# Warm-up matmuls, an earlier row load past a branch, a first block whose rows come a unit sooner, and small groups' weight loads spread two per block

## The chip, the cores and the metric

The kernel runs on one core of one Trainium2 chip. The metric is device time in microseconds (us) of one execution, lower is better. Five engines work side by side, each through its own list of instructions in order: TensorE (PE in the profile; PEld is its weight load), VectorE (DVE), ScalarE (ACT), GpSimd (POOL) and SyncE (SP), which here issues nearly all transfers between DRAM and the on-chip memory. ACTq, SPq and PEq are the engines' sequencers, which issue DMAs and take branches.

## The reference

Three layers follow one another on 4608 tokens of 512 values.

```python
# 1. linear attention: batch 8, heads 8, 576 tokens, head size 64, 128 features
proj = q_or_k @ w_phi                       # w_phi 64x128
proj = proj - max(abs(proj), axis=-1)
phi = concat([exp(proj), exp(-proj)])       # 256 features
kv = einsum('bhsf,bhsd->bhfd', phi_k, v); z = sum(phi_k, axis=seq)
num = phi_q @ kv; den = phi_q @ z + 1e-6    # attention = num / den -> x (4608, 512)
# 2. mixture of experts, top 1 of 8
logits = x @ w_gate + modality_bias[modality_id]
e_idx = argmax(logits); gate_w = softmax(logits)[e_idx]
for e in range(8):
    out[mask] = gate_w[mask] * (relu(x[mask] @ w1[e]) @ w2[e])   # w1 512x1024, w2 1024x512
# 3. a dense layer with a SoLU and a layer norm
h = out @ w_in                              # 512x1024
solu = h * softmax(h)
ln = (solu - mean(solu)) / sqrt(var(solu) + 1e-6) * g_ln
return ln @ w_out                           # 1024x512
```

## The kernel before

**Arithmetic.** Most products are made of three matmuls: each float32 operand is split into a high part (a rounding copy by ACT: `hi`, `whi`, `yTh`) and the low rest (a subtraction by DVE or POOL: `lo`, `wlo`, `yTl`), and high·high, low·high and high·low are added up (the helper at L1075 to L1078, `mm3`). An operand can be used once its copy and its rest are there.

**Stages.** The attention runs first, to some 430 us. ACT loads `w_phi` by two DMAs (L72, L73) and splits it (L76, L77); PE turns blocks of q and k (L255, `tp<-ident,ldk`), ACT and DVE split them (L258, L259), and L267 to L269 project them. Gates and routing write each token's row into `xe` in DRAM, sorted by expert. The experts work in nineteen units `u` = 0 to 18 of up to 256 rows. A unit's rows (`xin`) are read from `xe`, turned and split, multiplied with the first weights (`mm1`), passed through relu, multiplied with the second weights (`mm2`) and stored turned to `yd`. Its weights come as eight loads of 512 KB (`ldk`, `ldq`, `ldv`), asked for by SP in the order in which buffers come free, then split. Leftovers go into four small groups of 32 rows (`quad()`), of which each step multiplies with eight weight chunks' worth of a float32 copy without a split; their 24 later chunks are loaded by `load_mini`.

**Branch.** After units 0 and 1, `extras(0)` (L1468 to L1478) holds code for experts with too many rows. Its branch `tc.If(more > j)` is not taken with these inputs. Every engine must pass it; behind it SP waits for a buffer (`used((1, 7))`), loads the last chunk and then unit 3's rows (`m.load_x(3)`, L913, with the gates at L923).

**Dense layer.** The 36 tiles of 128 tokens go through `block()`: split of the next rows (`yT`, ACT L926 and POOL L927), the load of rows further on (`load_y`: `yin` L1226, `gt` L1228), `a3(n)` (24 matmuls of 128x512 with `win`, softmax, norm), turning of the result by DVE and a round trip through DRAM (`turned` L1244, `wlo` L1248, both issued by SP; the second waits for the first to land), `lnT` and the split of that (ACT `whi` L1297), and `a4`, the product with `w_out`, three tiles behind. `a3(0)` runs at the end of the last unit (u = 18, `NU-1`); then eight steps of `quad` stand between blocks, two blocks to a step. `w_in` and `w_out` are split by a generator `bg`, whose 66 steps are spread over `NPREP` uses of weights. The rows of the first two tiles are loaded with `load_y(0)` at the end of unit 17.

**Order.** PE's order is written by hand in the attention and from the units on; in the units the other engines' order is too. SP issues transfers in the order written there and stops at the first that must wait.

Of the kernel before, what the change touches and what calls it, by code (L numbers as in the profile page):

```python
# [39 lines left out]
COLS64 = 2  # L40
COLS32 = 1
TAIL = 1
BIAS = 8
BGN = 1
BGP = 100
PRE = 2
FSTEP = 2
RING = 5
RING0 = 1
STEP0 = 6  # L50
# [13 lines left out]
def setup_consts(nc, keep, pool, w_phi, w_gate):  # L64
    V, G = nc.vector, nc.gpsimd
    c = Consts()
    c.ident = keep.tile([P, P], F32, name="ident")
    make_identity(nc, c.ident)

# [1 line left out]
    V.memset(raw, 0.0)  # L71
    nc.scalar.dma_start(out=raw[0:D, 0:F], in_=w_phi)  # L72
    nc.scalar.dma_start(out=raw[D:P, F : 2 * F], in_=w_phi)  # L73
    c.wphi_hi = pool.tile([P, 2 * F], F32R, name="wphi_hi")
    c.wphi_lo = pool.tile([P, 2 * F], F32R, name="wphi_lo")
    nc.scalar.copy(c.wphi_hi, raw)  # L76
# [117 lines left out]
def attention(ctx, tc, c, cnt, xe, q, k, v, ld, early, m, late):  # L194
# [10 lines left out]
    kvp = ctx.enter_context(tc.tile_pool(name="a_kv", bufs=1, space=PSUM))  # L205

    ctx.enter_context(tc.manual_schedule(engines={mybir.EngineType.PE}))
    gd = [w1p.tile([P, 2, 4, 32], F32, name=f"gd{i}") for i in range(2)]
    for g_ in gd:
        V.memset(g_, 0.0)  # L210
# [745 lines left out]
def moe(ctx, m):  # L956
# [92 lines left out]
    def load_mini(i, g):  # L1049
        e, _, _, on = regs[NU + g]  # L1050
        m.load_raw(i, e, on != 0, i % 2 * NMINI + g)
# [3 lines left out]
    done = [RING0]  # L1055
    uses, steps_done = [0], [0]
    NSTEP = 4 * (2 * KD + KF) + 2
    NPREP = 8 * (START - 3) - 6

    def split_to(j):  # L1060
        while done[0] <= min(j, len(order) - 1):
# [170 lines left out]
    def yT(i):  # L1232
        hi = p2.tile([P, KD, P], F32R, name="yTh")
        lo = p2.tile([P, KD, P], F32R, name="yTl")
        m.split(ys[i][0], hi, lo, G)
        yt[i] = (hi, lo)
# [13 lines left out]
    def a3(i):  # L1250
        h = hps.tile([P, 2, 2, 2 * P], F32, name="h2").rearrange("p a b t -> p (a b t)")
        y = yt.pop(i)
        sc = lambda nm: p2.tile([P, 1], F32, name="s_" + nm)
        halves = [slice(n * 512, (n + 1) * 512) for n in range(2)]
        mxs = [sc("mx0"), sc("mx1")]
        for sl in halves:
            for k in range(KD):
                mm3(h[:, sl], both(y, lambda t: t[:, k, :]), both(win[k], lambda t: t[:, sl]), k == 0, k == KD - 1)
        for sl, mx in zip(halves, mxs):
            V.tensor_reduce(out=mx, in_=h[:, sl], axis=AX.X, op=ALU.max, negate=True)  # L1260
        g = ys[i][1]
        V.scalar_tensor_tensor(out=mx, in0=mx, scalar=mxs[0], in1=g, op0=ALU.min, op1=ALU.mult)
        ex = p1.tile([P, DFF], F32, name="ex")
        sm = sc("sm")
        A.activation(ex, h, AF.Exp, bias=mx, scale=g, accum_out=sm)  # L1265
        r = sc("r")
        V.tensor_scalar(out=r, in0=sm, scalar1=1e-9, scalar2=None, op0=ALU.add)
        V.reciprocal(r, r)
        tot = sc("tot")
        V.scalar_tensor_tensor(out=ex, in0=ex, scalar=r, in1=h, op0=ALU.mult, op1=ALU.mult, accum_out=tot)  # L1270
        for sl in halves:
            V.tensor_scalar(out=ex[:, sl], in0=ex[:, sl], scalar1=float(DFF), scalar2=tot, op0=ALU.mult, op1=ALU.subtract)  # L1272
        sq = p1.tile([P, DFF], BF16, name="sq")
        var = p2.tile([P, 1], F32, name="s_var")
        A.activation(sq, ex, AF.Square, accum_out=var)  # L1275
        rs = p2.tile([P, 1], F32, name="rs", bufs=5)
        g = ys[i][1]
        G.tensor_scalar(out=rs, in0=var, scalar1=g, scalar2=g, op0=ALU.mult, op1=ALU.mult)
        G.tensor_scalar(out=rs, in0=rs, scalar1=float(DFF) ** -3, scalar2=1e-6, op0=ALU.mult, op1=ALU.add)
        G.tensor_tensor(out=rs, in0=rs, in1=c.mhalf, op=ALU.pow)  # L1280
        G.tensor_scalar(out=rs, in0=rs, scalar1=g, scalar2=1.0 / DFF, op0=ALU.mult, op1=ALU.mult)
        st["rs", i] = rs
        st[i] = ex
        if i < NT - 1:
            st["lo", i] = lo = rp.tile([P, DFF], F32R, name="wlo")
            turn(i, ex, lo)
# [70 lines left out]
    def quad():  # L1357
        us = range(NU, NU + NMINI)
        group = lambda g: slice(g * MINI, (g + 1) * MINI)

        x = p1.tile([P, 2, DM], F32, name="xin")[:, 0, :]
        for g, u in enumerate(us):
            SP.dma_start(out=x[group(g)], in_=m.xe[bass.ds(regs[u][1], MINI), 0:DM])
            m.keep_gates(u)
        yield
        xt = blocks(x, KD, [m.xtp.tile([P, 4, P], F32, name="xTh")])[0]
        yield
        for i in range(4):
            if i % 2 == 0:
                b = bank.tile([P, 2, 2 * P], F32, name="tp")  # L1370
            for f in range(4):
                for g in range(NMINI):
                    T.matmul(
                        b[group(g), i % 2, :], lhsT=xt[:, f, group(g)], rhs=m.w1c(i % 2 * NMINI + g)[:, f, :],
                        start=i % 2 == f == 0, stop=f == 3, tile_position=(0, g * MINI), skip_group_check=True,
                    )
            for g in range(NMINI):
                load_mini(i + 2, g)
            if i % 2:
                A.activation(m.hr[:, i // 2 * 512 : i // 2 * 512 + 512], b.rearrange("p a f -> p (a f)"), AF.Relu)  # L1380
            yield
        ht = blocks(m.hr, KF, [p1.tile([P, 4, P], F32, name=f"hTh{n}") for n in range(2)])
        b = bank.tile([P, 2, 2 * P], F32, name="tp")
        yield
        for j in range(4):
            fh, dh = j // 2, j % 2
            for f in range(4):
                for g in range(NMINI):
                    T.matmul(  # L1389
                        b[group(g), dh, :], lhsT=ht[fh][:, f, group(g)], rhs=m.w1c(j % 2 * NMINI + g)[:, f, :],  # L1390
                        start=j == f == 0, stop=fh == 1 and f == 3, tile_position=(0, g * MINI), skip_group_check=True,
                    )
            if j < 2:
                for g in range(NMINI):
                    load_mini(j + 6, g)
            yield
        yr = p1.tile([P, DM], F32, name="yr")
        A.copy(yr, b.rearrange("p a d -> p (a d)"))
        yield
        yo = blocks(yr, KD, [p2.tile([P, 4, P], F32, name="yo")])[0]  # L1400

        def store(g, u):
            SP.dma_start(
                out=yd[:, m.cols(u)].rearrange("(c p) t -> p c t", p=P), in_=yo[:, :, group(g)]
            )
            slots[0] += g == NMINI - 1

        stores.extend(lambda g=g, u=u: store(g, u) for g, u in enumerate(us))
        yield
# [17 lines left out]

    def unit(u):
        gap(u)
        g = mm1(u)  # L1430
        for i in range(4):
            next(g)
            if i == XAT:
                run_mids()
                next_x(u)
                if u == NU - 2:
                    next(minis)
        run(g)
        gap(u)
        if u == NU - 2:  # L1440
            run(bg)
            load_y(0)
        if u == NU - 1:
            yT(0)
            next(minis)
            run_mids()
            block()
        run_mids()
        run(mm2([u]))

    with ExitStack() as sp:
        sp.enter_context(tc.manual_schedule(engines={mybir.EngineType.SP} | MANUAL))
        slot_regs(2, then=lambda: m.load_x(2, False))
        m.keep_gates(2)
        slot_regs(3)
        for ch in order[:RING0]:
            reload(*ch)
        split_to(LOOK)
        ln = tr(m.hr, ("yin", "ex"), p1)
        hT[0] = lambda f: both(ln, lambda t: t[:, f, :])  # L1460
        g = mm1(1)
        run(g)
        for i, _ in enumerate(mm2([0, 1])):
            if i == 2:
                m.xT(bank, 2)
        held = mids[:]
        mids.clear()
    more = nc.values_load(tab[0:1, 4:5], min_val=0, max_val=NEXTRA)  # L1468
# [12 lines left out]
    mids.extend(held)  # L1481
    ctx.enter_context(tc.manual_schedule(engines={mybir.EngineType.SP}))
    used((1, 7))
    m.load_x(3)
    slot_regs(4)
    nxt = [0, 0, 0]
    stores = []

    def block():
        n, split, done4 = nxt  # L1490
        run_mids()
        if n + 1 < NT:
            yT(n + 1)
            if n == 0:
                load_y(1)
            elif n % 2 and n + 3 < NT:
                load_y((n + 3) // 2)
            elif stores:
                stores.pop(0)()
        if n == NT - 1:  # L1500
            lnT(split)
        if n < NT:
            a3(n)
            nxt[0] += 1
        if split < n - 1:
            if n < NT - 1:
                lnT(split)
            nxt[1] += 1
        if done4 < n - 2:
            a4(done4)  # L1510
            nxt[2] += 1

    def gap(u):
        if u >= START:
            block()
# [105 lines left out]
```

## Time and profile before

| what | value |
| --- | --- |
| three runs, median | 1294.19 us (1291.05 to 1295.75) |
| profiled execution | 1293.31 us |
| its span in the trace | 1291.6 us (1.7 us lie around it) |
| mean granted clock of TensorE | 0.996 |
| busy PE / DVE / ACT / POOL | 98% / 67% / 52% / 31% |

The span runs from the first to the last instruction of the trace. A time in a row is counted from the span's start. Idle time of an engine stands in brackets behind the row of the instruction that ended it, with the one that released it.

### The profile page before, as it was taken

What the parts mean: (1) busy time and instruction counts of PE and PEld (TensorE: products, weight loads), DVE (VectorE), ACT (ScalarE), POOL (GpSimd) and SP (SyncE); (2) the same over time, 40 slices, a digit from 0 to 9 for tenths busy, and PEclk for the clock granted to TensorE, in tenths of its full rate; (3) what the DMA queues carried; (4) which work ended last, traced back from release to release, by engine and by line L of the source; (5) the groups of instructions that cost most, each with busy time, mean ns of one, the idle gap of its engine ahead of it and who ended that gap; (6) DMA issues with size and microseconds to landing.
All of it is one profiled execution on the core that took longest, in us unless ns stands there. A gap on an engine that the chain in (4) does not pass through costs nothing.

```text
span 1291.6 us, 25365 instructions
## 1 busy us (share of the span) xinstructions
PE 1260.4 (98%) x9242; PEld 1057.8 (82%) x9242; DVE 869.3 (67%) x1620; ACT 666.8 (52%) x1254; POOL 403.8 (31%) x479
## 2 busy tenths in 40 slices
PE   8999999999999989999999999999999999999997
PEld 7767777777766889999999999987777778888885
DVE  8757866876775848778878787747555555566562
ACT  5666666666665426555555555534334434444442
POOL 6655674674663200000000000013323323333331
PEclk9999999999999999999999999999999999999999
DMA  8711342232132222222623132477877875566542
GB/s 246 214 54 58 107 133 58 87 117 85 50 116 67 91 67 92 67 83 66 197 66 83 51 83 67 130 213 192 233 204 168 248 169 142 137 153 139 145 121 57
DMA packets 273760, 156.78 MB, mean 121 GB/s; under 512 B 181824, under 2 KB 255712, under 8 KB 273632
## 3 DMA queue, kind: packets, MB, share of 16 engines
q1 hardware_dynamic: 267648, 136.01, 39.3%
q0 software_dynamic: 5824, 19.04, 3.8%
q8 instruction: 75, 1.23, 0.4%
q14 instruction: 53, 0.43, 0.1%
q10 hardware_dynamic: 160, 0.07, 0.0%
HBM read 166.67 MB, written 51.37 MB: 169 GB/s over the span
## 4 chain that ended last, share of the span: by engine, by line
PE 53%; DMA 5%; SPq 2%; issue 1%; ACT 1%; DVE 1%; POOL 0%; POOLq 0%; ACTq 0%; DVEq 0%
PE tp L1078 26%; PE h L1078 25%; DMA turned<-whi 2%; PE tp L898 1%; DMA gd<-xe 1%; SPq L1248 1%; DMA wlo<-turned 1%; PE tp L1389 1%; SPq L884 1%; DMA yin<-yd 0%; ACT ex L1265 0%; DVE ex L1270 0%; DMA xin<-xe 0%; ACT whi L1297 0%; SPq L1228 0%
## 5 line engine op out<-in xcount | busy, mean ns | idle before, releaser
L322 POOL TENSOR_TENSOR es<-es,e 128x512 f32<-128x512 f32 x128 | 163.8, 1286 | 102.5 <-ACT e L278 90.9
L927 POOL TENSOR_TENSOR yTl<-yin,yTh 128x512 fp32r<-128x512 f32 x36 | 46.8, 1300 | 443.2 <-ACT yTh L926 442.1
L1078 PE MATMUL tp<-xTh,whi 128*128 128x256 f32 x432 | 121.7, 282 | 2.5 <-PEq L1470 2.1
L1078 PE MATMUL h<-hTl,whi 128*128 128x256 f32 x432 | 120.6, 279 | 0.4 <-DVE hTl L1093 0.4
L1078 PE MATMUL tp<-xTh,wlo 128*128 128x256 f32 x432 | 120.6, 279 | 0.0
L1078 PE MATMUL tp<-xTl,whi 128*128 128x256 f32 x432 | 120.5, 279 | 0.0
L1078 PE MATMUL h<-hTh,whi 128*128 128x256 f32 x432 | 120.5, 279 | 0.0
L1078 PE MATMUL h<-hTh,wlo 128*128 128x256 f32 x432 | 120.5, 279 | 0.0
L271 DVE TENSOR_REDUCE m<-mm 128x4 f32<-128x512 f32 x144 | 97.1, 681 | 15.9 <-PE mm L269 15.9
L259 DVE TENSOR_TENSOR lo<-tp,hi 128x512 fp32r<-128x512 f32 x72 | 49.6, 689 | 82.5 <-ACT hi L258 82.0
L1265 ACT ACTIVATE ex<-h,s_mx,gt 128x1024 f32<-128x1024 f32 x36 | 43.4, 1207 | 111.6 <-issue 56.8
L1260 DVE TENSOR_REDUCE s_mx<-h 128x1 f32<-128x512 f32 x72 | 46.3, 685 | 80.6 <-PE h L1078 80.6
L267 PE MATMUL mm<-wphi_hi,hi 128*128 128x256 f32 x288 | 94.2, 327 | 1.0 <-ACT hi L258 1.0
L1275 ACT ACTIVATE sq<-ex 128x1024 bf16<-128x1024 f32 x36 | 38.1, 1058 | 97.9 <-DVE ex L1272 97.9
L1078 PEld LDWEIGHTS tp<-xTh,whi 128*128 128x128 f32 x432 | 81.3, 188 | 2.9 <-issue 2.2
L338 ACT ACTIVATE qp<-tp 128x512 f32<-128x512 f32 x128 | 69.3, 597 | 25.8 <-PE tp L330 22.7
L1078 PEld LDWEIGHTS tp<-xTh,wlo 128*128 128x128 f32 x432 | 81.9, 190 | 0.0
L1078 PEld LDWEIGHTS h<-hTh,wlo 128*128 128x128 f32 x432 | 81.9, 190 | 0.0
L268 PE MATMUL mm<-wphi_lo,hi 128*128 128x256 f32 x288 | 81.6, 283 | 0.0
L1078 PEld LDWEIGHTS h<-hTl,whi 128*128 128x128 f32 x432 | 81.1, 188 | 0.6 <-DVE hTl L1093 0.6
L269 PE MATMUL mm<-wphi_hi,lo 128*128 128x256 f32 x288 | 81.4, 283 | 0.0
L1078 PEld LDWEIGHTS h<-hTh,whi 128*128 128x128 f32 x432 | 81.3, 188 | 0.0
(427 smaller groups left out, 3818.9 us busy)
## 6 DMA issues: line engine op xcount, KB each, us to landing
ldk<-in_moe_w_dram SPq DMA_DIRECT2D x66, 512.0 KB
ldv<-in_moe_w_dram SPq DMA_DIRECT2D x66, 512.0 KB
ldq<-in_moe_w_dram SPq DMA_DIRECT2D x44, 512.0 KB
turned<-whi SPq DMA_DIRECT2D x35, 512.0 KB
wlo<-turned SPq DMA_DIRECT2D x140, 128.0 KB
yd<-yo SPq DMA_DIRECT2D x36, 256.0 KB
yin<-yd SPq DMA_DIRECT2D x18, 512.0 KB
xin<-xe SPq DMA_DIRECT2D x16, 512.0 KB
```

The lines of the kernel that those rows point to most:

```text
L259: V.tensor_tensor(out=lo, in0=tp, in1=hi.bitcast(F32), op=ALU.subtract)
L267: T.matmul(o, lhsT=hi[:, 2 * a + j, :], rhs=c.wphi_hi, start=(j == 0), stop=False, skip_group_check=True)
L268: T.matmul(o, lhsT=hi[:, 2 * a + j, :], rhs=c.wphi_lo, start=False, stop=False, skip_group_check=True)
L269: T.matmul(o, lhsT=lo[:, 2 * a + j, :], rhs=c.wphi_hi, start=False, stop=True, skip_group_check=True)
L271: V.tensor_reduce(out=m, in_=pj, axis=AX.X, op=ALU.max, apply_absolute_value=True)
L322: G.tensor_tensor(out=eo, in0=eo, in1=ev[:, :, r, :], op=ALU.add)
L338: A.activation(u.qp[half][:, fh, 2 * hp : 2 * hp + 2, o : o + 2 * P], tp.rearrange("p (h r) t -> p h (r t)", r=2), AF.Exp, scale=sc,)
L927: eng.tensor_tensor(out=lo, in0=src, in1=hi.bitcast(F32), op=ALU.subtract)
L1078: T.matmul(o, lhsT=l, rhs=r, start=first and n == 0, stop=last and n == 2, skip_group_check=True)
L1260: V.tensor_reduce(out=mx, in_=h[:, sl], axis=AX.X, op=ALU.max, negate=True)
L1265: A.activation(ex, h, AF.Exp, bias=mx, scale=g, accum_out=sm)
L1275: A.activation(sq, ex, AF.Square, accum_out=var)
```

## The change

The change has six parts. (1) Twelve bf16 matmuls of zeros, 128x256, stand first on PE; DVE clears their operand (`warm`) first. (2) ACT copies one column of it (`early`), so that the load of its function table stands ahead of the two `w_phi` DMAs. (3) The list of constants that DVE works on between projections is started by another count (`BIAS`); in DVE's list the nine rows of it stand at the same place (71 and 72). (4) Unit 3's rows are asked for ahead of the branch, their gates still behind it. (5) `load_y(0)` stands at the end of unit 16 instead of 17 and the 66 splitting steps of `bg` are spread over 114 uses instead of 122; `yT(0)` stands at the start of the last unit; in `a3(0)` what is left in `mids` (pieces of turning and splitting) is run between the two halves of 12 matmuls. (6) The small groups' loads go into a list, from which each block takes two, where four were issued at once behind a step.

```diff
-BIAS = 8
+BIAS = 14
+WARM = 12
 ...
+    c.warm = pool.tile([P, 2 * P], BF16, name="warm")
+    V.memset(c.warm, 0.0)
 ...
     nc.scalar.dma_start(out=raw[0:D, 0:F], in_=w_phi)
     nc.scalar.dma_start(out=raw[D:P, F : 2 * F], in_=w_phi)
+    early = pool.tile([P, 64], F32, name="early")
+    nc.scalar.copy(early[:, 0:1], c.warm[:, 0:1])
 ...
     ctx.enter_context(tc.manual_schedule(engines={mybir.EngineType.PE}))
+    warm = mmp.tile([P, 4, F], F32, name="mm").rearrange("p a f -> p (a f)")[:, 0 : 2 * P]
+    for n in range(WARM):
+        T.matmul(warm, lhsT=c.warm[:, 0:P], rhs=c.warm, start=True, stop=True, skip_group_check=True)
 ...
-    NPREP = 8 * (START - 3) - 6
+    NPREP = 8 * (START - 4) - 6
 ...
-        for sl in halves:
+        for n, sl in enumerate(halves):
+            if i == 0 and n:
+                run_mids()
             for k in range(KD):
                 mm3(h[:, sl], both(y, lambda t: t[:, k, :]), both(win[k], lambda t: t[:, sl]), k == 0, k == KD - 1)
 ...
-            for g in range(NMINI):
-                load_mini(i + 2, g)
+            feed.extend((i + 2, g) for g in range(NMINI))
 ...
             if j < 2:
-                for g in range(NMINI):
-                    load_mini(j + 6, g)
+                feed.extend((j + 6, g) for g in range(NMINI))
 ...
     def unit(u):
         gap(u)
+        if u == NU - 1:
+            yT(0)
 ...
-        if u == NU - 2:
+        if u == NU - 3:
             run(bg)
             load_y(0)
         if u == NU - 1:
-            yT(0)
             next(minis)
-            run_mids()
-            block()
+            block(False)
         run_mids()
 ...
+        m.load_x(3, False)
         held = mids[:]
 ...
-    m.load_x(3)
+    m.keep_gates(3)
 ...
-    def block():
+    def block(mid=True):
         n, split, done4 = nxt
-        run_mids()
+        if mid:
+            run_mids()
 ...
             a3(n)
             nxt[0] += 1
+            for x in [feed.pop(0) for _ in range(2) if feed]:
+                load_mini(*x)
```

Line numbers of the changed kernel are a few higher (L255 becomes L263, L884 becomes L892, L1078 becomes L1086, L1226 becomes L1234, L1470 becomes L1481). ACT's list at the very start (`wphi_raw` is `w_phi` as loaded, `hi` the high part of a turned block), before:

```order
L72 DMA wphi_raw<-in_w_phi_dram 64x128
L73 DMA wphi_raw<-in_w_phi_dram 64x128
L76 ACT_TABLE_LOAD
L76 CAST wphi_hi<-wphi_raw 128x256
L258 CAST hi<-tp 128x512 x3
```

and after:

```order
L78 ACT_TABLE_LOAD
L78 CAST early<-warm 128x1
L75 DMA wphi_raw<-in_w_phi_dram 64x128
L76 DMA wphi_raw<-in_w_phi_dram 64x128
L81 CAST wphi_hi<-wphi_raw 128x256
L266 CAST hi<-tp 128x512 x3
```

The table load moved from behind the two DMAs to ahead of them. SP's list behind the branch (`ldk` is a weight chunk, `xin` unit 3's rows, `gd` gates), before:

```order
L1470 UNCONDITIONAL_BRANCH x2
L884 ISA
L884 REGISTER_ALU
L884 ISA
L884 DMA ldk<-in_moe_w_dram 128x4x256
L913 ISA
L913 DMA xin<-xe 128x2x512
L923 ISA
L923 DMA gd<-xe 256x2
```

and SP's list ahead of the same branch, after:

```order
L892 ISA
L892 REGISTER_ALU
L892 ISA
L892 DMA ldv<-in_moe_w_dram 128x4x256
L921 ISA
L921 DMA xin<-xe 128x2x512
L1481 COMPARE_AND_BRANCH
```

The rows' load moved past the branch and past the weight chunk `ldk`. PE's list in the last unit (`whi,xTl` ends `mm1` of unit 18, `xin` are the small groups' rows, `tp<-ident,ldq` turns relu's result of unit 18, `h` is `a3(0)`), before:

```order
L1078 MATMUL tp<-whi,xTl 128x256
L1320 MATMUL tp<-ident,xin 128x128 x4
L1115 MATMUL tp<-ident,ldq 128x128 x8
L1078 MATMUL h_12838<-win0h,yTh 128x512
L1078 MATMUL h_12838<-win0l,yTh 128x512
L1078 MATMUL h_12838<-win0h,yTl 128x512
L1078 MATMUL h_12838<-win1h,yTh 128x512
```

and after, from the end of the first half of `a3(0)` on:

```order
L1086 MATMUL h_12837<-win3h,yTh 128x512
L1086 MATMUL h_12837<-win3l,yTh 128x512
L1086 MATMUL h_12837<-win3h,yTl 128x512
L1123 MATMUL tp<-ident,ldq 128x128 x8
L1086 MATMUL h_12837<-win0h,yTh 128x512
L1086 MATMUL h_12837<-win0l,yTh 128x512
L1086 MATMUL h_12837<-win0h,yTl 128x512
```

The eight turning matmuls moved from ahead of the 24 to between the halves. SP's list in the stretch of the small groups (`turned` and `wlo` are the two legs of the round trip), before:

```order
L884 DMA ldk<-in_moe_w_dram 128x4x256
L884 ISA
L884 REGISTER_ALU
L884 ISA
L884 DMA ldv<-in_moe_w_dram 128x4x256
L1226 DMA yin<-yd 128x4x256
L1228 DMA gt<-gd 128x2x2
L1244 DMA turned_6220<-whi 128x1024
L1248 DMA wlo<-turned_6220 32x32x32 x4
L1244 DMA turned_6221<-whi 128x1024
L1248 DMA wlo<-turned_6221 32x32x32 x4
```

and after:

```order
L1236 DMA gt<-gd 128x2x2
L1252 DMA turned_6237<-whi 128x1024
L1256 DMA wlo<-turned_6237 32x32x32 x4
L892 ISA
L892 REGISTER_ALU
L892 ISA
L892 DMA ldv<-in_moe_w_dram 128x4x256
L892 ISA
L892 REGISTER_ALU
L892 ISA
L892 DMA ldk<-in_moe_w_dram 128x4x256
L1252 DMA turned_6238<-whi 128x1024
```

Two of the four loads moved from ahead of the first round trip to between the first and the second.

## Rows read from the trace of the kernel before

**Rows 1.** The page, busy time of the engines: us (share) x instructions.

```profile
PE 1260.4 (98%) x9242; PEld 1057.8 (82%) x9242; DVE 869.3 (67%) x1620; ACT 666.8 (52%) x1254; POOL 403.8 (31%) x479
```

**Rows 2.** Waits of PE: what waited, its releaser: us, times, longest.

```profile
PE tp L255 <- DMA ldk<-in_k_dram: 4.0, 1, 4.0
PE tp L1078 <- ACT whi L1297: 2.9, 4, 1.7
PE tp L898 <- DMA xin<-xe: 2.2, 1, 2.2
...
PE h L1078 <- ACT yTh L926: 1.7, 1, 1.7
```

**Rows 3.** Timeline of the start: start, us, engine, line, operation [idle before, releaser].

```profile
1.82 0.61 ACTq L73 DMA_DIRECT2D wphi_raw<-in_w_phi_dram  x1
...
5.16 1.28 ACT L76 ACT_TABLE_LOAD   x1 [5.16 <-DMA wphi_raw<-in_w_phi_dram]
...
6.46 0.41 ACT L76 CAST wphi_hi<-wphi_raw 128x256 fp32r<-128x256 f32 x1
...
7.40 0.58 PE L267 MATMUL mm<-wphi_hi,hi 128*128 128x256 f32 x1 [0.99 <-ACT hi L258]
...
10.09 0.41 PE L268 MATMUL mm<-wphi_lo,hi 128*128 128x256 f32 x1
10.30 0.42 PE L269 MATMUL mm<-wphi_hi,lo 128*128 128x256 f32 x1
...
14.87 0.28 PE L268 MATMUL mm<-wphi_lo,hi 128*128 128x256 f32 x1
14.98 0.28 PE L269 MATMUL mm<-wphi_hi,lo 128*128 128x256 f32 x1
```

**Rows 4.** Windows: length, busy PE, PEld, DVE, ACT, POOL, granted clock, DMA, GB/s.

```profile
7.40:14.00 6.60, 6.58 (x29) 6.28 (x30) 6.50 (x33) 2.06 (x4) 1.99 (x10) 1.00 0.98 245
...
478.21:481.62 3.41, 3.41 (x19) 3.41 (x17) 0.00 (x0) 0.00 (x0) 0.00 (x0) 0.50 0.40 47
...
853.68:857.09 3.41, 3.41 (x9) 2.64 (x9) 0.33 (x1) 0.02 (x1) 1.28 (x1) 0.50 1.09 377
```

**Rows 5.** Timeline around the branch, SP's queue and then PE.

```profile
467.57 0.07 SPq L884 DMA_DIRECT2D ldv<-in_moe_w_dram  x1
473.44 0.08 SPq L884 DMA_DIRECT2D ldk<-in_moe_w_dram  x1
473.72 0.40 SPq L913 DMA_DIRECT2D xin<-xe  x1
...
469.00 0.36 PE L1078 MATMUL tp<-xTh,whi 128*128 128x256 f32 x1 [2.05 <-PEq L1470]
...
477.34 1.19 PE L898 MATMUL tp<-ident,xin 128*128 128x128 f32 x8 [2.19 <-DMA xin<-xe]
```

**Rows 6.** Timeline of the last unit, first tile of the dense layer.

```profile
844.68 0.50 SPq L1226 DMA_DIRECT2D yin<-yd  x1
...
851.10 0.62 ACT L926 CAST yTh<-yin 128x512 fp32r<-128x512 f32 x1 [0.37 <-DMA yin<-yd]
...
851.77 0.50 PE L1078 MATMUL h<-win0h,yTh 128*128 128x512 f32 x1 [1.73 <-ACT yTh L926]
...
853.17 0.50 PE L1078 MATMUL h<-win0h,yTl 128*128 128x512 f32 x1 [0.67 <-POOL yTl L927]
```

**Rows 7.** Timeline of the small groups' stretch, SP's queue and one row of PE.

```profile
909.25 0.50 SPq L1244 DMA_DIRECT2D turned<-whi  x1
916.81 2.79 SPq L1248 DMA_DIRECT2D wlo<-turned  x4
...
958.13 1.03 SPq L1244 DMA_DIRECT2D turned<-whi  x1
967.30 2.82 SPq L1248 DMA_DIRECT2D wlo<-turned  x4
...
974.00 0.50 PE L1078 MATMUL tp<-wout0h,whi 128*128 128x512 f32 x1 [1.72 <-ACT whi L1297]
```

More of the change, by code (lines that the diff above doesn't have):

```diff
@@ L1370, in quad @@
                 b = bank.tile([P, 2, 2 * P], F32, name="tp")
+            assert all(x[0] > i for x in feed)
             for f in range(4):
@@ L1386, in quad @@
             fh, dh = j // 2, j % 2
+            assert all(x[0] > j + 4 for x in feed)
             for f in range(4):
@@ L1483, in moe @@
     used((1, 7))
-    m.load_x(3)
+    m.keep_gates(3)
     slot_regs(4)
     nxt = [0, 0, 0]
-    stores = []
-    def block():
+    stores, feed = [], []
+    def block(mid=True):
         n, split, done4 = nxt
-        run_mids()
+        if mid:
+            run_mids()
         if n + 1 < NT:
```

## The prediction, made before the changed kernel had run

> **What bounds the kernel now.** I read the page's busy times first: PE is busy for 1260.4 us of the 1291.6 us span, DVE for 869.3, the rest less [rows 1]. So the time is PE's list from end to end plus its gaps, and a faster DVE, ACT or POOL is worth only what it takes out of a gap. Second, the list of PE's waits: of the 31 us in which PE is idle, the large single waits are the first transfer (4.0), the second operand of the third layer's output product (2.9 in four waits, the longest 1.7), unit 3's rows (2.2) and the split of the first tile's rows (1.7) [rows 2]. Beside these stands only the branch, where PE waits 2.05 us for its own sequencer [rows 5]; no other single wait is as long as 1.3 us. Third, the timeline at each of these gaps, to see which instruction is late and what it stands behind [rows 3, 5, 6, 7]. Fourth, the windows just behind the gaps, because a gap has a second price: in 478.21 to 481.62 and in 853.68 to 857.09, both right after a gap, the granted clock is 0.50, PE's lower level of 1.2 GHz [rows 4]. Work that takes 3.41 us at 1.2 GHz takes 1.7 us at 2.4 GHz, so each such stretch costs 1.7 us more than the gap shows. PE's work itself is not reduced by the change (twelve small matmuls are added, while PE has nothing to do), so the most that can be had is the gaps that it touches, with their slow stretches: some 12 to 14 us.
>
> **Part by part.** All terms are differences to the profiled execution's 1293.31 us, which is its span of 1291.6 and 1.7 around it; the median of the runs is 0.9 higher.
>
> *Warm-ups and the early table load.* PE waits 4.0 us for the first rows whatever is done [rows 2], so twelve short matmuls fit into that wait as soon as DVE has cleared their operand. Two things may follow. First the table load: it takes 1.28 us at 5.16, behind the `w_phi` DMA, and the cast starts right behind it at 6.46 [rows 3]. Ahead of the DMAs it costs nothing by itself, but ACT's list now issues the DMAs behind it. The second DMA was issued at 1.82 and landed at 5.16, 3.34 us later. If ACT's queue is held until the table load is over, it is issued 1.3 us later and lands at about 6.5: no gain. If it isn't held, the cast starts at 5.2: a gain of 1.3. I take the middle, 0.7. Second the clock: the projections' matmuls start 0.21 us apart at 10.09 and 0.11 us apart at 14.87 [rows 3], so from 7.40 to 14.00 PE runs at its lower level by its spacing, although the window's column shows 1.00 there. At the higher level its 6.6 us of work would take 3.3. But DVE is busy 6.50 of these 6.60 us [rows 4], and PE's products feed DVE, which hands the next operands back: the clock alone gives no more than the 0.1 that DVE has free, unless part of DVE's work there can wait, as the constants do. I take 0.2. Sum −0.9; bounds +0.5 (DMAs late, warm-ups in the way of the first turning matmuls) to −3.3 (PE alone decides).
>
> On the table load the Trainium skill (page "ScalarE: Activation LUTs", section "What ACT_TABLE_LOAD costs") puts a drain of some 1380 ns behind the 1283 ns of the load. The row agrees with the load (1.28) and not with the drain, since the cast follows 0.02 us after it. By the page the sum would be up to 1.4 us lower; I go by the row.
>
> *Unit 3's rows ahead of the branch.* SP issues its last transfer before the branch at 467.57, the next ones at 473.44 (the weight chunk, which waits for its buffer) and 473.72 (the rows), and PE starts to turn the rows at 477.34, 3.6 us behind the issue, after 2.19 us idle [rows 5]. Issued at about 468, the rows land at about 472; PE wants them at 477.34 − 2.19 = 475.15, so 3 us are left. The 2.19 goes. The stretch at 1.2 GHz behind it goes with it if it was this gap that brought it, 1.7. The 2.05 us at the branch itself stay [rows 5]. What is late next: the turned rows' split on ACT and DVE, which do nothing at all in the 3.41 us behind 478.21 [rows 4] and so can take it at once. Sum −3.9; bounds 0 (the buffer comes free only there) to −3.9.
>
> *First block.* `yin` is issued at 844.68, as late as SP reaches it, lands at 851.10, and PE waits 1.73 us for `yTh` and 0.67 for `yTl` [rows 6], then runs 3.41 us at 1.2 GHz [rows 4]. Asked for a unit earlier, the rows are there some 23 us sooner (sixteen units, 2 to 17, lie between 469 and 847) and the split stands at the start of the last unit; it takes ACT 0.62 us [rows 6] and POOL 1.28 [rows 4], beside PE's weights work. That is 1.73 + 0.67 + 1.7 = 4.1. What is late next is relu's turned result: its eight turning matmuls now stand behind twelve of the 24, so that PE has 12 matmuls of 0.23 us, some 2.8 us, to cover what ACT has to do first. Sum −4.1; bounds −1.0 (the split of the turned result, or the second tile's rows, takes the gap's place) to −4.1. The 66 splitting steps are pressed into 114 uses instead of 122, 7% more densely on DVE, at 67% busy; I count +0.5 for single waits that they bring, bounds 0 to +1.5.
>
> *Small groups' loads.* In this stretch PE is not ahead of SP: of each pair of round trips the first waits from 909.25 to 916.81, 7.6 us, or from 958.13 to 967.30, 9.2 us, for the turned block to land, and PE then waits for its split, 1.72 us at 974.00 [rows 7], 2.9 us in all [rows 2]. Four loads of 512 KB stand ahead of the first trip of a pair and none ahead of the second. With two ahead of each, the long wait gets shorter and the short one longer; the bytes are the same. The gaps come from the long one, so most of 2.9 should go: −2.0; bounds +3 (both trips become middling and SP gets no faster over the pair) to −2.9.
>
> Sum: −0.9 − 3.9 − 4.1 + 0.5 − 2.0 = −10.4, so 1293.3 − 10.4 = **1282.9 us**.
>
> **Rivals.** *The gaps are only handed on.* For: PE's list is 98% full, and each row moved earlier lands on a queue that had something else to do; the branch still stops every engine for 2.05 us; in the last unit, turning, split and rows crowd on ACT, DVE and POOL. Against: behind 478.21 ACT and DVE are not busy at all for 3.41 us, behind 853.68 for 0.02 and 0.33 of 3.41 [rows 4], so there is room. Half of the 10.4 would go: about 1288.
>
> *Nothing is gained.* The rows' buffer (`xin`) may be read until shortly before its load was issued, then the early load waits on SP ahead of the branch, with the weight chunk and everything behind it; the first tile's rows may wait for the stores of unit 17. With the last unit's minimum of 1.0, the tail at 0 and the start at 0: 1290 to 1294. Against: SP issued its seven transfers before the branch without a stop, the last at 467.57 [rows 5].
>
> *Slower: weight chunks of the small groups come late.* A step of the small groups needs four chunks. The last two of them are now issued a block later than before, behind a round trip. From there to the step that needs them lie two blocks, about 25 us (916.81 to 967.30 is four blocks, 50.5 us). The round trip ahead of them takes 7.6 us and 2.8 to issue [rows 7], the landing some 6.4 as `yin` did [rows 6]: 16.8, so 8.4 are left. It decides from the point at which SP falls more than 8.4 us further behind PE; then each of six refills stops PE for some 4 us (a gap of 2.3 and a 1.7 us slow stretch), +24 − 10 is 1307. For: SP has hardly any slack in this stretch. Against: the loads are spread, which evens SP's waits.
>
> *The slow clock comes anyway.* The granted clock stood at 1.00 through the branch's own 2.05 us and fell only after the second gap [rows 4, 5]; without that second gap it may still fall behind the first. Then 1.7 comes back: 1284.6, inside my range. The Trainium skill (page "TensorE: Matmul & The Clock Gate", section "What's actually happening") says that the half rate is the default, that activity releases it, and that the moment differs from run to run. The trace agrees in that both stretches at the lower level stand behind gaps; one execution doesn't show how much the moment varies. By that rule the same goes for the warm-ups, which end before PE's pause of 0.99 us ahead of 7.40 [rows 3]: they could then buy nothing, which changes 0.2 of my sum.
>
> **How the numbers follow.** The forecast, with the clock rival inside it, has 66%: 1279.5 to 1285.5 by itself, from the terms' near bounds. Handed on, 1285.5 to 1290: 18%. Nothing gained, 1290 to 1294: 9%. Slower, above 1300: 7%. The range 1279.0 to 1289.5 leaves out the last two and a little at the lower end, where the start's full 3.3 and the tail's 2.9 would come together. About 0.5%, 6.5 us, is what a measurement of this kernel can tell from no change. Below 1287.7 lies the forecast and half of the second case: 0.75. Within it lie the other half and the third: 0.18. Slower: 0.07.
>
> **What would show it.** In the new profile: the rows' load `xin` stands in SP's queue at about 468, and the turning of unit 3's rows has no idle time before it; the granted clock is 1.00 from 475 to 485. In the last unit the first `h` matmul waits for nothing, and the clock stays up there. In the small groups' stretch the waits from `turned` to `wlo` are all near 6 us, and PE's waits for `whi` sum to under 1 us. At the start the matmuls are 0.11 us apart from the first projection, but the end of the attention's first head moves by under 1 us. I am wrong if PE's busy time grows, if waits for `hTl`, `xTl` or the small groups' chunks appear in PE's list, or if the refills make PE wait.

## The result: 1.4% slower

The changed kernel is slower: the ratio to the kernel before is 1.0137, with a 95% interval of 1.0115 to 1.0158, or 17.7 us. Its executions took 1309.6, 1309.9 and 1314.0 us (a fourth was disturbed at 2085.6 and is left out), the profiled one 1309.93 with a span of 1307.9. The forecast was 1282.9 us with a range of 1279.0 to 1289.5, so the time lies outside the range, on the other side. What came was the rival with a 7% chance: the small groups' chunks are late.

First the page's busy times and PE's list of waits in the changed kernel, which answer to [rows 1, 2] (columns: us in total, times, longest):

```profile
PE 1266.5 (97%) x9254; PEld 1061.1 (81%) x9254; DVE 864.0 (66%) x1621; ACT 666.1 (51%) x1255; POOL 405.6 (31%) x479
```

```profile
PE tp L1384 <- DMA ldv<-in_moe_w_dram: 11.3, 2, 10.5
...
PE tp L1086 <- PEq L1481: 2.0, 1, 2.0
PE h L1086 <- ACT whi L934: 1.9, 1, 1.9
PE tp L1384 <- DMA ldk<-in_moe_w_dram: 1.6, 2, 0.9
PE tp L1176 <- ACT yr L1171: 1.3, 1, 1.3
```

The four waits of [rows 2] are gone (that for `ldk` because the warm-ups now fill it). In their place stand one of 10.5 us for a small group's chunk, and new ones for `whi` and `yr`; the branch's 2.0 is as before [rows 5]. PE is also busy 6.1 us longer, of which the warm-ups are 2.7. Five landmarks in PE's timeline tell where the 16.3 us of span went (the turning of a unit's rows, and the first output product of the dense layer's tiles 0 and 35):

| stretch of PE's list | before, us | after, us | difference | term of the forecast |
| --- | --- | --- | --- | --- |
| start to unit 2's turning | 461.68 | 462.37 | +0.7 | −0.9 |
| unit 2's to unit 4's turning (the branch) | 39.97 | 41.82 | +1.9 | −3.9 |
| unit 4's to unit 18's turning | 324.64 | 327.78 | +3.1 | +0.5 |
| unit 18's turning to tile 0's output product | 60.81 | 57.79 | −3.0 | −4.1 |
| tile 0's to tile 35's output product | 389.77 | 403.37 | +13.6 | −2.0 |

Of the four gains that were forecast only the fourth row's came. The last row is the result. SP's queue and PE in the small groups' stretch of the changed kernel, beside [rows 7]:

```profile
872.10 0.40 PE L1384 MATMUL tp<-ldk,xTh 128*32 128x256 f32 x1
...
881.40 0.40 PE L1384 MATMUL tp<-ldq,xTh 128*32 128x256 f32 x1
...
898.84 0.39 SPq L892 DMA_DIRECT2D ldk<-in_moe_w_dram  x1
899.66 0.39 SPq L892 DMA_DIRECT2D ldq<-in_moe_w_dram  x1
...
901.25 0.62 SPq L1252 DMA_DIRECT2D turned<-whi  x1
908.24 2.87 SPq L1256 DMA_DIRECT2D wlo<-turned  x4
911.53 0.58 SPq L892 DMA_DIRECT2D ldv<-in_moe_w_dram  x1
912.57 0.39 SPq L892 DMA_DIRECT2D ldk<-in_moe_w_dram  x1
...
906.37 0.40 PE L1384 MATMUL tp<-ldk,xTh 128*32 128x256 f32 x1
...
917.48 1.06 PE L1384 MATMUL tp<-ldv,xTh 128*32 128x256 f32 x2 [10.49 <-DMA ldv<-in_moe_w_dram]
...
919.25 0.64 PE L1384 MATMUL tp<-ldk,xTh 128*32 128x256 f32 x2 [0.71 <-DMA ldk<-in_moe_w_dram]
```

The small groups' first two steps begin at 872.10 and 881.40, the third at 906.37 with the two chunks issued at 898.84 and 899.66. The other two stand behind a round trip for which SP waits from 901.25 to 908.24; they are issued at 911.53 and 912.57, after PE already stands still, and land 6 to 6.7 us later. The windows show the second price (columns as in [rows 4]):

```profile
906.60:917.40 10.80, 0.39 (x4) 0.00 (x0) 2.52 (x3) 3.27 (x6) 4.01 (x6) 0.73 0.78 199
...
917.48:924.90 7.42, 6.71 (x33) 3.23 (x34) 0.00 (x0) 0.00 (x0) 0.00 (x0) 0.50 0.46 114
```

PE does nothing for the wait and then runs at 1.2 GHz for 7.4 us, its 6.7 us of work costing 3.4 more. Wait 11.2, clock 3.4, and 1.7 of waits at the fourth step (two, near 948) are 16.3 of the 17.0 us by which tile 0 to tile 4 takes longer (66.81 instead of 49.77). Some of it comes back, since behind a later PE the round trips are on time: from tile 4 to tile 8 it takes 47.15 us instead of 50.57, and the wait of 1.72 at [rows 7] is gone.

### The profile page after: what moved, and what is told of

Same layout as the page of the kernel before. It is cut to its first block, busy times and chain, and to the rows that moved or that the text cites. A ratio compares the mean times of both kernels' runs of the same rounds, so it can differ in the third digit from the quotient of the medians.

```text
span 1307.9 us, 25379 instructions
## 1 busy us (share of the span) xinstructions
PE 1266.5 (97%) x9254; PEld 1061.1 (81%) x9254; DVE 864.0 (66%) x1621; ACT 666.1 (51%) x1255; POOL 405.6 (31%) x479
## 4 chain that ended last, share of the span: by engine, by line
PE 53%; DMA 3%; DVE 3%; ACT 1%; SPq 1%; issue 1%; POOL 0%; POOLq 0%; ACTq 0%; DVEq 0%
PE tp L1086 26%; PE h L1086 25%; PE tp L906 1%; DVE wlo L935 1%; DMA turned<-whi 1%; SPq L1256 1%; DMA yin<-yd 1%; PE tp L1400 1%; DMA ldk<-in_moe_w_dram 1%; DMA yd<-yo 0%; ACT whi L934 0%; PE tp L1384 0%; DMA ldv<-in_moe_w_dram 0%; SPq L892 0%; DVE ex L1280 0%
## 5 line engine op out<-in xcount | busy, mean ns | idle before, releaser
L1086 PE MATMUL tp<-xTh,whi 128*128 128x256 f32 x432 | 122.8, 284 | 3.4 <-PEq L1481 2.0
L1086 PE MATMUL h<-hTh,whi 128*128 128x256 f32 x432 | 120.7, 279 | 1.9 <-ACT whi L934 1.9
L1086 PE MATMUL tp<-xTh,wlo 128*128 128x256 f32 x432 | 121.4, 281 | 0.0
L1086 PE MATMUL h<-hTh,wlo 128*128 128x256 f32 x432 | 120.7, 279 | 0.8 <-DVE wlo L935 0.8
L1086 PE MATMUL h<-hTl,whi 128*128 128x256 f32 x432 | 120.8, 280 | 0.6 <-DVE hTl L1101 0.6
L1086 PE MATMUL tp<-xTl,whi 128*128 128x256 f32 x432 | 121.3, 281 | 0.0
L1288 POOL TENSOR_SCALAR rs<-s_var,gt 128x1 f32<-128x1 f32 x36 | 12.3, 341 | 250.8 <-ACT sq L1285 250.8
L1086 PEld LDWEIGHTS tp<-xTh,whi 128*128 128x128 f32 x432 | 82.2, 190 | 4.3 <-issue 2.2
L1086 PEld LDWEIGHTS h<-hTh,whi 128*128 128x128 f32 x432 | 81.4, 188 | 2.1 <-ACT whi L934 2.1
L1086 PEld LDWEIGHTS h<-hTh,wlo 128*128 128x128 f32 x432 | 81.8, 189 | 1.0 <-DVE wlo L935 1.0
L1086 PEld LDWEIGHTS tp<-xTh,wlo 128*128 128x128 f32 x432 | 82.5, 191 | 0.0
L1086 PEld LDWEIGHTS tp<-xTl,whi 128*128 128x128 f32 x432 | 82.0, 190 | 0.0
L1086 PEld LDWEIGHTS h<-hTl,whi 128*128 128x128 f32 x432 | 81.2, 188 | 1.0 <-DVE hTl L1101 1.0
```

The costliest lines, as they stand in the source:

```text
L1086: T.matmul(o, lhsT=l, rhs=r, start=first and n == 0, stop=last and n == 2, skip_group_check=True)
```

## The experiments

Kernels that ran together shared a chip and the runs of the kernel before. That kernel took 1294.05 us on the first chip, 1300.8 and 1300.2 beside the later ones, so results are given as ratios with their 95% intervals; stretches are read from each one's own trace.

**Four loads at once in the changed kernel.**

```diff
-            feed.extend((i + 2, g) for g in range(NMINI))
+            for g in range(NMINI):
+                load_mini(i + 2, g)
 ...
             if j < 2:
-                feed.extend((j + 6, g) for g in range(NMINI))
+                for g in range(NMINI):
+                    load_mini(j + 6, g)
```

> The changed kernel with one part undone: the small groups' loads are again issued four at once behind a step. Theory A (the late chunks at 917.48, with their 10.5 us wait and the slow clock behind it, are all that the small groups' part cost): PE's waits for ldv and ldk chunks go, the tail after the last unit is as in the kernel before or a little later (the 1.7 us wait for whi comes back), so about 14 us less than the changed kernel, 1297 to 1299 us. Rival B (the chunks come late because the last unit ended sooner and the loads would be late four at once too): PE still waits 5 us or more for a chunk, 1305 us or more.

1.0016 (0.9999 to 1.0032), 1295.98 us, 1 us below what theory A expects. Its mechanism holds: no wait for a chunk is left in PE's list, and tile 0 to tile 35 takes 388.93 us. The waits for `whi` that it expects back are not there. The difference to the changed kernel is 1.2% or 15.6 us. Its SP queue and PE:

```profile
892.00 0.40 SPq L892 DMA_DIRECT2D ldk<-in_moe_w_dram  x1
...
894.38 0.37 SPq L892 DMA_DIRECT2D ldk<-in_moe_w_dram  x1
...
895.48 2.32 SPq L1252 DMA_DIRECT2D turned<-whi  x1
904.08 2.79 SPq L1256 DMA_DIRECT2D wlo<-turned  x4
...
906.01 0.40 PE L1384 MATMUL tp<-ldk,xTh 128*32 128x256 f32 x1
```

All four chunks are issued by 894.38, ahead of the round trip, 11.6 us before PE wants them at 906.01.

**Two loads per block in the kernel before.** Part 6 alone.

> The kernel before with the small groups' loads two per block, and nothing else. Theory A: the third step's last two chunks stand behind one more round trip, PE waits about 10 us for them and runs slowly behind it, some +13.5 us: 1306 to 1309 us. Rival B (it takes the other parts to make them late): at most +2 us, 1292 to 1296, with no wait of PE for a chunk above 2 us.

1.0119 (1.0084 to 1.0153), 1310.61 us. Theory A again, a little above its range: a wait of 10.75 us, one of 1.61 and tile 0 to tile 35 in 404.04 us. This part alone makes the loss, whatever the last unit does.

**Two loads, but ahead of the round trip**, in the changed kernel.

```diff
     def block(mid=True):
 ...
+        for x in [feed.pop(0) for _ in range(2) if feed]:
+            load_mini(*x)
         if n + 1 < NT:
             yT(n + 1)
 ...
             a3(n)
             nxt[0] += 1
-            for x in [feed.pop(0) for _ in range(2) if feed]:
-                load_mini(*x)
```

> The changed kernel with one thing moved: the two loads that a block takes from the list are issued at the block's start, ahead of its rows and its round trip, and not behind its a3. Theory A' (what makes the chunks late is that they stand behind round trips for which SP waits 7 us each; the number per block doesn't matter): the third step's first two chunks are issued at about 888 instead of 899 and the last two at about 899 instead of 912, one round trip sooner, landing around 905 to 907 where PE wants them at 906.4. PE waits 0 to 2 us for chunks and never slows down: 1296 to 1300 us. Rival B' (two per block are too few whatever their place): PE still waits over 5 us at the third step and the time stays above 1304 us.

1.0018 (1.0008 to 1.0028), as with four at once. Everything on this chip stands 7.8 us later, as the third step's start (914.13 instead of 906.37) shows:

```profile
911.75 0.82 SPq L892 DMA_DIRECT2D ldv<-in_moe_w_dram  x1
912.99 0.38 SPq L892 DMA_DIRECT2D ldk<-in_moe_w_dram  x1
...
916.42 0.62 PE L1384 MATMUL tp<-ldv,xTh 128*32 128x256 f32 x2 [1.67 <-DMA ldv<-in_moe_w_dram]
917.87 0.41 PE L1384 MATMUL tp<-ldk,xTh 128*32 128x256 f32 x2 [0.83 <-DMA ldk<-in_moe_w_dram]
```

The last two chunks are issued 2.4 us before the step and not 5.2 behind it, so 7.5 us sooner: one round trip's wait. The waits shrink to 1.67 and 0.83 us, and the clock stays up. The place in SP's queue is what counts, not two or four. The round trips are even here, 6.1 to 7.5 us each from 900.9 to 989.4, where the kernel before has 3.9 to 9.2 from 892.0 to 970.2; it gains nothing, since tile 0 to tile 35 takes 389.54 us instead of 389.77.

**Unit 3's rows ahead of the branch**, in the kernel before: part 4 alone.

> The kernel before with unit 3's rows asked for ahead of the branch, and nothing else. Theory C (SP passes the branch only when every transfer that it issued ahead of it has landed, so the rows' 4 to 5 us hold back the whole branch): ACT's first instruction behind the branch about 3 us later (473 to 474 instead of 470.6), the weight chunk behind it issued 3 us later, PE waits near 491 for whi and wlo, and unit 4's rows are turned 1.5 to 2 us later than before (503 instead of 501.65): 1294 to 1297 us. Rival D (the forecast): 1289 to 1291, ACT's first instruction where it was.

1.0028 (1.0008 to 1.0048), 1298.03 us, some 3.6 us slower, 1 us above what theory C expects. The branch in the changed kernel, SP's queue, ACT's first instruction behind it and where PE waits later:

```profile
468.30 0.07 SPq L892 DMA_DIRECT2D ldv<-in_moe_w_dram  x1
468.98 0.40 SPq L921 DMA_DIRECT2D xin<-xe  x1
476.35 0.08 SPq L892 DMA_DIRECT2D ldk<-in_moe_w_dram  x1
...
473.90 1.05 ACT L934 CAST whi<-ldk 128x1024 fp32r<-128x1024 f32 x1 [6.61 <-SPq L1481]
...
492.11 0.38 PE L1086 MATMUL h<-hTh,whi 128*128 128x256 f32 x1 [1.94 <-ACT whi L934]
493.37 0.38 PE L1086 MATMUL h<-hTh,wlo 128*128 128x256 f32 x1 [0.76 <-DVE wlo L935]
```

In the kernel before the same cast of ACT stands 2.99 us behind SP's last issue (`ldv` at 467.57, [rows 5]):

```profile
470.56 1.05 ACT L926 CAST whi<-ldk 128x1024 fp32r<-128x1024 f32 x1 [3.98 <-SPq L1470]
```

Here it stands 4.92 us behind the rows' issue, and SP's next chunk 7.4 behind it. In all kernels without the move the distance is 2.98 to 3.23 us, in all four with it 4.86 to 5.00. But the two are not alike. A unit's weight chunks are loaded only under a condition (`cond` in `load_raw`), and those at the branch move nothing: their issue takes 0.07 us instead of 0.4, and from 467.6 to 473.5 the DMA queues of the kernel before (`--dma`: packets, MB, share) carry instructions alone:

```profile
q8 instruction: 2, 0.03, 2.3%
q14 instruction: 3, 0.02, 1.3%
```

So the 2.99 us are the branch with no transfer of SP's under way. Counted from the last chunk's issue, ACT's cast comes 2.6 us later with the rows ahead of the branch (5.60 instead of 2.99): 1.0 us for issuing them, and 1.5 because SP's first step behind its branch comes 3.90 to 4.05 us after it, in the four kernels with the rows, and 2.43 to 2.68 in the other eight. The landing of the rows doesn't end that wait: by the trace's records their last piece lands 3.39 us after the branch in two of the four, 0.6 before SP goes on, and 3.97 and 4.02 after it in the others, when SP has gone on already. In all twelve traces SP's step comes 1.07 to 1.30 us behind the end of an 8 KB transfer of instructions (`q14`), which starts 2.30 to 2.43 us after the branch with the rows and 0.88 to 1.12 without. So SP looks to wait for code; whether the rows' traffic or another place of the code makes that later, no run separates.

The wait of 2.19 us that the move takes away is handed on to 492.11: unit 2's to unit 4's turning takes 41.8 to 43.4 us with the move, 39.8 to 41.0 where nothing of unit 3 is asked for ahead of the branch. Of part 4's own 43.4, 1.7 are a second stretch of 3.41 us at 1.2 GHz, behind those waits (494.85 to 498.27).

**Unit 3's rows behind the branch, ahead of the chunk**, in the kernel before.

```diff
-    used((1, 7))
-    m.load_x(3)
+    m.load_x(3)
+    used((1, 7))
```

> The kernel before with unit 3's rows asked for behind the branch but ahead of the weight chunk that waits for its buffer, and nothing else. Theory C: the branch is passed as before (ACT's first instruction at about 470.6), the rows are issued at about 470.7 instead of 473.72 and land at about 474.5, so PE's wait of 2.19 us for them goes, with or without the slow stretch behind it: 2 to 4 us less, 1290 to 1292 us. Rival D (what follows behind unit 3's rows, the chunk and its split, is what is late anyway): no change, a new wait of about 2 us for whi or wlo near 490.

1.0003 (0.9990 to 1.0017): no difference, a miss for theory C's time. Rival D has the time right, but its new wait near 490 isn't there. ACT's cast comes 3.00 us behind the last issue, as before:

```profile
469.78 0.07 SPq L884 DMA_DIRECT2D ldv<-in_moe_w_dram  x1
...
472.78 1.04 ACT L926 CAST whi<-ldk 128x1024 fp32r<-128x1024 f32 x1 [4.00 <-SPq L1470]
...
475.14 0.40 SPq L913 DMA_DIRECT2D xin<-xe  x1
...
480.55 1.09 PE L898 MATMUL tp<-ident,xin 128*128 128x128 f32 x8 [1.28 <-DMA xin<-xe]
```

But SP itself issues the rows only 2.4 us after that, 5.36 behind its last issue, where it took 6.15 before [rows 5]. So 0.8 us was to be had and not 3: the branch held the rows (SP's last step in it is at 474.83), not the chunk's buffer, and PE still waits 1.28.

**Unit 3's gates instead of its rows ahead of the branch**, in the kernel before: `m.keep_gates(3)` ahead of it, `m.load_x(3, False)` behind it.

> The kernel before with unit 3's gates (2 KB) and not its rows (512 KB) asked for ahead of the branch; the rows stay behind it. Theory C (the branch is passed when the last transfer ahead of it has landed, be it wanted or not): ACT's first instruction behind the branch comes later than the 3.0 us behind the last chunk's issue that it takes in the kernel before, by about the time that the gates need to land (some 2 us from an issue 0.7 us later): 472 instead of 470.6 if units start as before; 1294 to 1297 us. Rival D' (it is the rows' buffer or size, not the branch): ACT's first instruction 3.0 us behind the last chunk's issue as before, 1293 to 1295 us.

1.0013 (1.0004 to 1.0022), some 1.7 us slower. The gates are 2 KB and nobody wants them soon, yet ACT's cast stands 4.83 us behind the last chunk's issue instead of 3.0:

```profile
478.36 0.07 SPq L884 DMA_DIRECT2D ldv<-in_moe_w_dram  x1
479.10 0.61 SPq L923 DMA_DIRECT2D gd<-xe  x1
...
483.19 1.05 ACT L926 CAST whi<-ldk 128x1024 fp32r<-128x1024 f32 x1 [5.83 <-SPq L1471]
```

Of the 1.8 us, 1.3 are SP's time for issuing them. The rest is mostly a wait as theory C has it: SP's third step behind the branch comes at 482.92, 0.41 us behind the second, and the gates' last piece lands at 482.91. So a transfer ahead of the branch can hold it until it lands, as here; for the rows something else took longer. PE's own wait at the branch stays 2.0 to 2.4 us in all kernels; its wait for unit 3's rows is 3.72 us here instead of 2.19.

**The first block's part alone**, in the kernel before: part 5 alone.

> The kernel before with the first block's part alone (its rows loaded a unit sooner, split at the start of the last unit, the turning between the halves, the splitting steps over 114 uses). Forecast's term: the gaps of 1.73 and 0.67 us before the first block and the slow stretch of 3.41 us behind them go, 4.1 less and 0.5 more: 1290 to 1291 us. Rival (the gap is handed on): a wait of 1.1 to 1.9 us of PE for yr (the units' last result, split later now) and 0.5 for yTl behind it, as in the changed kernel, and the first output product of the dense layer only 2.5 to 3 us sooner; of that the small groups' stretch may give back 0 to 2: 1291 to 1293 us.

1.0010 (0.9997 to 1.0022): no gain, below the rival's hope too. The last unit did gain: unit 18's turning to tile 0's output product takes 58.54 us, between 57.8 and 58.6 in all four kernels with the part as changed, 60.0 to 62.5 in those without it. The units before lost it: unit 4's to unit 18's turning takes 327.23 us, 326.0 to 327.8 in the four, 323.8 to 325.5 without. PE's waits between 500 and 840 in this kernel:

```profile
PE tp L1078 <- DVE hTl L1093: 0.9, 2, 0.7
PE h L1078 <- DVE hTl L1093: 0.6, 2, 0.4
```

Four waits for DVE's split, where the kernel before has one of 0.4 us in this stretch. They sum to 1.5 us, and each of the four units is longer than its like by more than its wait: by 0.9, 0.5, 0.6 and 1.25 us, 3.3 in all (with the one of before among them).

**The same with the splitting steps over 122 uses.**

```diff
-    NPREP = 8 * (START - 4) - 6
+    NPREP = 8 * (START - 3) - 6
```

> The kernel before with the first block's part alone, as in the earlier run of that part, but the 66 splitting steps spread over 122 uses as before and not 114; what is left of them after unit 16 (some four steps) is then done at once. Theory E (the denser steps make DVE late with hTl in units 4 to 17, three waits more and a slower unit behind each, 2.3 us that eat what the last unit gains): between the turning of unit 4's and of unit 18's rows it takes 324 to 325.5 us again instead of 326.0 to 327.8, with one or two waits for hTl; the last unit keeps its gain of about 3: 1.5 to 2.5 us less than the kernel before of the same chip. Rival F (moving the rows and the split is what disturbs the units, or the four steps done at once cost as much): 326 us or more, and no difference to before.

1.0001 (0.9986 to 1.0017). Theory E in the units, 0.1 us above the range that it gives: 325.62 us and a single wait, the one of before:

```profile
PE h L1078 <- DVE hTl L1093: 0.4, 1, 0.4
```

But the last unit's gain is gone with it: 61.00 us, with a wait of 2.95 us for `yr` and 3.41 us at 1.2 GHz behind it, from 883.06, which cost 1.7 more. Rival F is right about the time. Whether the steps done at once made that wait wasn't separated.

**The same, and the rows ahead of the chunk.**

> The same with unit 3's rows asked for behind the branch but ahead of the weight chunk, as a candidate for a faster kernel: if both are as measured alone and add up, 2 to 3 us less than the kernel before; if theory E is wrong or the stretch of the small groups gives it back, no difference.

0.9990 (0.9974 to 1.0007): no difference that can be measured. In this trace a wait of 2.9 us for `yr` and one of 3.0 for `yTh` stand among PE's waits. No version that ran beats the kernel before.

**The start alone**: parts 1 to 3 in the kernel before.

> The kernel before with the twelve warm-up matmuls, the early table load and the other count for the constants, and nothing else. Forecast's term: 0.9 less, 1293 us. Rival (DVE sets the pace of the first head, and what the start gains is waited off later in the attention): the first projection at 7.2 instead of 7.4, matmuls 0.11 us apart there, but unit 2's rows turned at the same time as before within the 3 us by which this time differs between runs of one kernel: 1293 to 1296 us, not to be told from before.

0.9999 (0.9987 to 1.0011): nothing. The start in the changed kernel, beside [rows 3]:

```profile
0.81 1.28 ACT L78 ACT_TABLE_LOAD   x1 [0.81 <-PEq L1620]
...
1.96 0.61 ACTq L76 DMA_DIRECT2D wphi_raw<-in_w_phi_dram  x1
...
6.21 0.41 ACT L81 CAST wphi_hi<-wphi_raw 128x256 fp32r<-128x256 f32 x1 [3.92 <-DMA wphi_raw<-in_w_phi_dram]
...
7.16 0.58 PE L275 MATMUL mm<-wphi_hi,hi 128*128 128x256 f32 x1 [0.73 <-ACT hi L266]
...
12.88 0.28 PE L275 MATMUL mm<-wphi_hi,hi 128*128 128x256 f32 x1
12.99 0.28 PE L276 MATMUL mm<-wphi_lo,hi 128*128 128x256 f32 x1
```

The table load is out of the way and ACT's queue was not held by it (the second DMA at 1.96, during the load), but the data landed 4.25 us later instead of 3.34, so the cast begins 0.25 sooner. The clock's rise, the first record of the clock in either trace, comes at 10.35 us instead of 14.00. At 12.88 the matmuls are 0.11 us apart, at 10.09 of [rows 3] they were 0.21, and then PE waits for DVE (0.43 us for `xsq` at 13.81). By 342.58 both kernels stand at the same time to 0.01 us.

## Why the prediction was wrong, point by point

**Small groups' loads: −2.0 forecast, +13.6 in the profile, +15.4 alone.** This is the step that failed, twice. The term counted the same bytes before each round trip and looked at PE's waits for `whi`; it didn't ask when PE needs the chunks that were moved back. And the slower rival, which did ask, gave them two blocks, 25 us together, between issue and use and so 8.4 us to spare. The third step has only one block between: the first two steps stand close together on PE (872.10 and 881.40 in the changed kernel, one block between them where later steps have two), so the list holds both steps' chunks at once, and the last two of the third step's come out a block before they are needed, behind a wait of 7 us. Instead of 8.4 us to spare they were issued 5.2 us late. Its price was mis-sized too: one refill at 11.2 + 3.4 and one at 1.7, not six at 4, since a PE that is once held back stays behind. The bounds of the term (+3 to −2.9) left this out, and the chance of 7% was far too small for a queue of which the text itself says that it has hardly any slack. Nor did the 2.9 us of waits for `whi` that were to go belong to the four loads at once: PE's lists have none to 1.8 us of them in the eight other kernels that load four at once.

**Unit 3's rows: −3.9 forecast, +1.9 in the profile, +3.6 alone.** The rows were issued at 469 and were there for PE, as forecast; the wait of 2.19 went. What failed is the claim that this costs nothing. ACT's first cast behind the branch waits for SP's own way past it, and with the rows ahead it comes 2.6 us later behind the last chunk's issue; PE then waits 1.94 us for `whi` and 0.76 for `wlo`. That this comes from SP at the branch is shown, why SP's pause there is longer is open. The prediction took the transfers ahead of the branch for loads ("without a stop" [rows 5]); they move nothing, so they told nothing of what 512 KB would do. The slow stretch was not had either: in the changed kernel the clock is at 0.50 from 471.15 to 474.57, behind the branch's own 2.04 us:

```profile
471.16:474.56 3.40, 3.40 (x18) 3.40 (x17) 0.00 (x0) 0.66 (x1) 0.00 (x0) 0.50 0.30 110
```

That is the rival "the slow clock comes anyway", and here it is right: the second gap went and the slow stretch stayed. Each of the other traces has one, too, somewhere between 471 and 504 us. The Trainium skill (page "TensorE: Matmul & The Clock Gate", section "What's actually happening") says that activity releases the half rate and that the moment differs from run to run. No run here shows that for one kernel, since each has one trace; between kernels the place differs, since the same gap of 2.05 brought no slow stretch in the kernel before [rows 4, 5].

**First block: −4.1 forecast, −3.0 measured; denser steps: +0.5 forecast, +1.4 to +3.1 measured.** The two gaps before the first block and the slow stretch behind them went as forecast. A quarter of the gain was handed on; PE waits for `yr` (1.27) and `yTl` (0.51) in their place. The denser steps are the mis-sized term: DVE at 67% on the mean is late at single places, and four such waits cost twice their own sum.

**Start: −0.9 forecast, 0 measured.** DVE set the pace, as argued, and what little was gained was waited off later.

**Rivals.** "Only handed on" is what happened to the first block, "slower" to the small groups' loads. The argument that two loads each even out SP's waits is right where they stand ahead of the trip (6.1 to 7.5 us each), and it gained nothing.

## What to carry to other kernels

When loads are moved back in an in-order queue, work out for each the time at which its user wants it and the time at which the queue reaches it, with every blocking wait ahead of it, and do this for the tightest use and not for the regular one. A transfer issued just ahead of a branch can be part of the branch's price, even where nobody wants its data. And a change of several parts is best costed by its worst part: here the start, the rows and the first block each came to about nothing to +3.6 us, and the small groups' loads to 15.

## What was not expected of the hardware

- SP's last issue ahead of the branch and ACT's first work behind it are tied: 2.98 to 3.23 us where that issue moves nothing, 4.09 for 2 KB of gates, 4.86 to 5.00 for 512 KB of rows. SP's own pause there ends 1.07 to 1.30 us behind a transfer of instructions in all twelve traces; only with the gates does SP then wait for a landing, too.
- Units of the same some 200 matmuls, without a wait and at a granted clock of 1.00, take either 22.66 us or 23.49, in every trace, with matmuls 0.113 or 0.118 us apart. They mostly alternate, and behind a wait a unit can take the longer time. What decides was not settled; it moves the sum over the units by up to 0.8 us for each.
- The Trainium skill (page "ScalarE: Activation LUTs", section "What ACT_TABLE_LOAD costs") counts some 1380 ns of drain with each switch to another set of tables. Each execution here has one table load, its first, and no drain shows behind it: in the changed kernel, too, ACT's next instruction stands 0.01 us behind the load's end (2.10 after 0.81 + 1.28). A switch between two sets no run here shows.
- The granted clock's column can miss a slow start: from 7.16 to 14.00 it shows 1.00 in the changed kernel, while the matmuls up to 9.97 are 0.21 us apart; the first record of the clock in that trace stands at 10.35.
